# A hand-written order for every engine in an attention and maxout-FFN kernel, with padded queries and the first batch masked on VectorE

## The chip, the cores and the metric

The kernel runs on one core of a Trainium2 chip. The metric is the device time of one execution in microseconds, the median of several runs. "Span" is the first to the last instruction in the profiled execution; it is about 2 us shorter than the timed value.

## The reference, cut to what matters

```python
B, H, S, Nb, D = (8, 8, 576, 16, 64)          # causal attention, 16 beacon keys ahead of 576
scores = where(causal, -1e9, scale * q @ k_all^T)
attn   = softmax(scores) @ v_all              # 8 batches of 8 heads
x = attn.transpose(0, 2, 1, 3).reshape(4608, 512)
h = max(x @ w1, x @ w2, x @ w3)               # 768 wide
out = h @ w_out
```

Inputs and output are fp32; the kernel computes in bf16 with fp32 accumulation.

## The kernel before

Heads are taken in pairs. For one pair TensorE transposes q and k (12 and 16 small matmuls), then computes the scores k by q in 12 matmuls (six pieces, two heads). ScalarE takes the exponential out of PSUM, GpSimd writes zeros over the masked part, and after two pairs (a quad) TensorE runs six PV passes of 20 matmuls, each on a quarter of the array's columns. Part 0 of each half gives the softmax sums, which ScalarE turns into reciprocals with Ln and Exp. The FFN works on blocks of 512 tokens: 18 units of four matmuls (mm1) and four units of six (mm2). There are 32 pairs, 96 PV passes and 198 FFN units, and 4064 matmuls in all.

```python
def emit_scores(hp, q_sb, k_sb, at_sb, j0):
    # ... 12 transposes into qT_ps (score pool), VectorE copies to qT
    # ... 16 transposes into kT_ps (score pool), VectorE copies each head's half to a zero-padded kT
    for t in range(n_kt):
        for r0, r1 in groups:
            for e in range(2):
                nc.tensor.matmul(ps[...], kTf[e][...], qT[:, r0:r1, p0:QP], start=True, stop=True)
            for e in range(2):
                nc.scalar.activation(out=at_sb[...], in_=sc[e][...], func=AF.Exp, scale=scale)
        for e in range(2):
            nc.gpsimd.affine_select(out=view, in_=view, ...)     # causal mask, every batch
# ... emit_pv, emit_mm1, emit_mm2

loads = {0: emit_loads(0, H // 2)}       # every load is issued by GpSimd
emit_weight_loads()                      # 24 + 1 loads
loads[1] = emit_loads(1, 1)
for b in range(B):
    if b + 2 < B:
        loads[b + 2] = emit_loads(b + 2, 1)
    for g in range(2):
        # ... scores of two pairs, then emit_pv
    with tc.high_priority(offset=-(10**6)):        # the scheduler fills FFN in where it can
        for tb in blocks_after[b]:
            # ... mm2 of the block before, mm1 of this one
```

A scheduler fixes the order of each engine's instructions when the program is built, taking attention first and FFN where attention would wait. PSUM has three score buffers (also used by the transposes), two PV buffers and three FFN buffers.

The softmax here doesn't subtract the row's maximum and nothing guards it: scores larger than these inputs give would overflow.

## Time and profile before

| | before |
|---|---|
| timed, median of 3 | 419.08 us (418.48 to 420.77) |
| span | 417.2 us |
| TensorE busy | 365.0 us (87%) |
| next busiest, VectorE and ScalarE | 45%, 44% |

First, from the profile page of before, the busy time of each engine, and TensorE's busy share and granted clock in tenths over 40 equal slices of the span.

```profile
span 417.2 us, 9759 instructions
...
PE 365.0 (87%) x4024; PEld 187.9 (45%) x4064; DVE 188.4 (45%) x311; ACT 185.4 (44%) x503; POOL 170.8 (41%) x432
...
PE   3871159999999999999799999999999999999994
...
PEclk9999999999999999999999999999999999999998
...
```

TensorE's holes lie in the first seven slices. The windows view of before has three stretches: start-up, attention with FFN, FFN alone. Its columns are the stretch and its length, then busy microseconds (and instructions) of PE, PEld, DVE, ACT and POOL, then granted TensorE clock, DMA share and GB/s.

```profile
...
0.00:63.00 63.00, 29.56 (x279) 14.76 (x283) 12.84 (x24) 17.82 (x52) 48.62 (x97) 1.00 1.26 137
63.00:313.00 250.00, 237.50 (x3308) 128.94 (x3332) 122.86 (x211) 151.23 (x424) 122.17 (x336) 1.00 0.43 55
313.00:409.00 96.00, 94.79 (x434) 42.95 (x441) 50.00 (x74) 16.39 (x28) 0.00 (x0) 1.00 0.16 45
...
```

TensorE is the busy engine, but busy time is not streaming time: an FFN matmul is shown 380 ns long in the trace, and the next one starts after 216 ns. I therefore use the starts of successive matmuls. FFN to FFN is 216 ns at 512 (median). I count a matmul of N columns as N x 0.417 + 2.5 ns of streaming, a line that lies within 3 ns of all of these. A quarter of that counts for PV (in before, a group of four at 288 columns starts 122 ns ahead of the next group, and one at 234 columns 99 ns; the line gives 122.6 and 100.1), half for transposes (two of 96 columns in 43 ns, where the line gives 42.5); the medians of two PV or two transposes in a row lie within 13 ns of this count. By this count the whole kernel streams for 283 us. What a start-to-start time has beyond that I call a gap.

Next, the waits view of before for TensorE: who waited for whom, microseconds in total, how often, and the longest in microseconds.

```profile
...
PE sc L144 <- DMA q_sb<-in_q_dram: 12.8, 2, 8.1
PE pv L222 <- POOL at_sb L196: 9.2, 3, 7.3
PE sc L154 <- DMA k_sb<-in_beacon_k_dram: 4.9, 2, 3.6
...
```

The timeline of before at start-up, TensorE's and GpSimd's lines of it (start, duration, engine, line, operation; in brackets the idle time ahead and what ended it):

```profile
...
29.02 0.45 PE L178 MATMUL sc<-qT,kT_104 128*128 128x288 bf16 x1
29.25 0.45 PE L178 MATMUL sc<-qT,kT_106 128*128 128x288 bf16 x1
...
31.02 2.65 POOL L133 DMA_DIRECT2D v_sb<-in_v_dram  x3
...
37.20 0.88 POOL L133 DMA_DIRECT2D v_sb<-in_v_dram  x1 [3.53 <-DMA w_out_sb<-in_moe_w_out_dram]
...
40.63 0.69 PE L144 MATMUL sc<-ident,q_sb 96*64 96x96 bf16 x12 [8.11 <-DMA q_sb<-in_q_dram]
...
44.94 0.71 PE L154 MATMUL sc<-ident,k_sb 74*64 74x74 bf16 x16 [3.61 <-DMA k_sb<-in_beacon_k_dram]
...
46.08 0.78 POOL L114 DMA_DIRECT2D q_sb<-in_q_dram  x1 [4.47 <-issue]
...
54.10 0.73 POOL L133 DMA_DIRECT2D v_sb<-in_v_dram  x1 [1.85 <-DMA q_sb<-in_q_dram]
54.84 10.98 POOL L196 TENSOR_SCALAR_AFFINE_SELECT at_sb<-at_sb 128x114 bf16<-128x114 bf16 x40
55.26 0.67 PE L222 MATMUL pv<-at_sb,ones 128*32 128x288 bf16 x2 [7.28 <-POOL at_sb L196]
...
```

Between 32 and 55 us TensorE waits for batch 1's q, then its k, then for the mask of batch 0. In GpSimd's line the 40 selects of the mask (L196) stand behind its load issues for batches 1 and 2, which go on until 54.8 us. Between them are holes of 3.53 and 1.85 us that the trace puts down to earlier transfers; for the one of 4.47 us it names no cause.

### The profile page before, as it was taken

What the parts mean: (1) busy time and instruction counts of PE and PEld (TensorE: products, weight loads), DVE (VectorE), ACT (ScalarE), POOL (GpSimd) and SP (SyncE); (2) the same over time, 40 slices, a digit from 0 to 9 for tenths busy, and PEclk for the clock granted to TensorE, in tenths of its full rate; (3) what the DMA queues carried; (4) which work ended last, traced back from release to release, by engine and by line L of the source; (5) the groups of instructions that cost most, each with busy time, mean ns of one, the idle gap of its engine ahead of it and who ended that gap; (6) DMA issues with size and microseconds to landing.
All of it is one profiled execution on the core that took longest, in us unless ns stands there. A gap on an engine that the chain in (4) does not pass through costs nothing.

```text
span 417.2 us, 9759 instructions
## 1 busy us (share of the span) xinstructions
PE 365.0 (87%) x4024; PEld 187.9 (45%) x4064; DVE 188.4 (45%) x311; ACT 185.4 (44%) x503; POOL 170.8 (41%) x432
## 2 busy tenths in 40 slices
PE   3871159999999999999799999999999999999994
PEld 1430026545455454555545455455544444444441
DVE  3230103465354645545455363454545555555543
ACT  2661006565656557556574665755562121212120
POOL 8993588646625736644562523424230000000000
PEclk9999999999999999999999999999999999999998
DMA  7999996918729904960780300001200303030303
GB/s 97 146 173 177 123 109 90 88 20 112 53 64 148 61 2 62 125 91 6 116 58 11 93 3 2 2 2 39 65 2 2 101 0 102 0 101 2 101 0 102
DMA packets 61005, 27.65 MB, mean 66 GB/s; under 512 B 43168, under 2 KB 56352, under 8 KB 60960
## 3 DMA queue, kind: packets, MB, share of 16 engines
q0 software_dynamic: 55200, 17.58, 40.5%
q1 hardware_dynamic: 5760, 9.44, 8.0%
q8 instruction: 32, 0.52, 0.5%
q14 instruction: 13, 0.11, 0.1%
HBM read 35.13 MB, written 9.44 MB: 107 GB/s over the span
## 4 chain that ended last, share of the span: by engine, by line
PE 72%; POOL 9%; DMA 7%; ACT 5%; issue 3%; DVE 3%; SPq 0%; POOLq 0%; DVEq 0%
PE fps L248 33%; PE pv L222 13%; PE sc L178 12%; PE fps L266 11%; DMA k_sb<-in_k_dram 4%; ACT lnd L232 3%; POOL at_sb L196 3%; PE sc L144 2%; POOL v_sb L133 2%; POOL w_sb L99 2%; DMA q_sb<-in_q_dram 2%; DVE xT L237 2%; PE sc L154 1%; ACT recip L234 1%; DMA w_sb<-in_moe_w_dram 1%
## 5 line engine op out<-in xcount | busy, mean ns | idle before, releaser
L186 ACT ACTIVATE at_sb<-sc 128x288 bf16<-128x288 f32 (+4 forms) x384 | 129.1, 418 | 73.0 <-PE sc L178 70.5
L248 PE MATMUL fps<-xT,w_sb 128*128 128x512 bf16 x619 | 156.8, 380 | 3.3 <-issue 2.7
L196 POOL TENSOR_SCALAR_AFFINE_SELECT at_sb<-at_sb 128x132 bf16<-128x132 bf16 (+2 forms) x320 | 96.1, 324 | 107.1 <-ACT at_sb L186 101.1
L258 DVE TENSOR_TENSOR hT<-hT,fps 128x512 bf16<-128x512 bf16 x108 | 74.3, 688 | 77.2 <-PE fps L248 56.0
L248 PEld LDWEIGHTS <-w_sb 128*128 128x128 bf16 x648 | 60.9, 98 | 64.8 <-issue 3.6
L256 ACT CAST hT<-fps 128x512 bf16<-128x512 f32 x54 | 31.6, 584 | 86.7 <-PE fps L248 85.3
L222 PE MATMUL pv<-at_sb,v_sb 128*32 128x234 bf16 (+4 forms) x1280 | 62.1, 244 | 3.8 <-ACT lnd L232 2.4
L266 PE MATMUL fps<-w_out_sb,hT 128*128 128x512 bf16 x205 | 52.3, 379 | 2.2 <-issue 1.1
L222 PE MATMUL pv<-at_sb,ones 128*32 128x234 bf16 (+4 forms) x640 | 42.1, 249 | 11.8 <-POOL at_sb L196 9.2
L150 DVE COPY qT<-sc 128x576 bf16<-128x576 bf16 x32 | 14.6, 457 | 78.5 <-PE sc L144 73.7
L222 PEld LDWEIGHTS <-v_sb 128*32 128x32 bf16 (+1 forms) x1280 | 36.7, 98 | 15.4 <-issue 10.3
L237 DVE TENSOR_TENSOR xT<-pv,recip 128x288 bf16<-128x288 f32 x64 | 26.5, 453 | 37.4 <-ACT recip L234 36.4
L232 ACT ACTIVATE lnd<-pv 128x288 f32<-128x288 f32 x32 | 13.1, 410 | 58.0 <-PE pv L222 58.0
L133 POOL DMA_DIRECT2D v_sb<-in_v_dram x40 | 33.7, 860 | 8.2 <-DMA q_sb<-in_q_dram 4.6
L222 PEld LDWEIGHTS <-ones 128*32 128x32 bf16 (+1 forms) x640 | 20.6, 97 | 34.2 <-issue 27.0
L274 DVE COPY y<-fps 128x512 f32<-128x512 f32 x36 | 24.5, 691 | 23.1 <-PE fps L266 21.6
L144 PE MATMUL sc<-ident,q_sb 96*64 96x96 bf16 x384 | 20.7, 223 | 12.8 <-DMA q_sb<-in_q_dram 12.8
L266 PEld LDWEIGHTS <-hT 128*128 128x128 bf16 x216 | 20.4, 98 | 22.2 <-DVE hT L258 2.1
L154 PE MATMUL sc<-ident,k_sb 74*64 74x74 bf16 x512 | 20.5, 209 | 6.4 <-DMA k_sb<-in_beacon_k_dram 4.9
L144 PEld LDWEIGHTS <-q_sb 96*64 96x64 bf16 x384 | 13.2, 116 | 21.4 <-DMA q_sb<-in_q_dram 13.1
L178 PE MATMUL sc<-qT,kT_104 128*128 128x288 bf16 (+2 forms) x66 | 20.3, 308 | 1.8 <-DVE kT_104 L163 1.7
L178 PE MATMUL sc<-qT,kT_108 128*128 128x288 bf16 (+2 forms) x66 | 19.9, 301 | 1.8 <-DVE kT_108 L163 1.7
(38 smaller groups left out, 238.3 us busy)
## 6 DMA issues: line engine op xcount, KB each, us to landing
out_dram<-y SPq DMA_DIRECT2D x24, 192.0 KB, 2.4
q_sb<-in_q_dram POOLq DMA_DIRECT2D x7, 576.0 KB, 6.1
k_sb<-in_k_dram POOLq DMA_DIRECT2D x7, 576.0 KB, 9.7
v_sb<-in_v_dram POOLq DMA_DIRECT2D x24, 128.0 KB, 4.9
out_dram<-y SPq DMA_DIRECT2D x24, 128.0 KB, 2.4
w_sb<-in_moe_w_dram POOLq DMA_DIRECT2D x24, 96.0 KB, 4.0
out_dram<-y SPq DMA_DIRECT2D x24, 64.0 KB, 2.0
v_sb<-in_v_dram POOLq DMA_DIRECT2D x8, 112.0 KB, 4.0
```

Source lines behind the costliest of these rows:

```text
L133: nc.gpsimd.dma_start(out=v_sb[lo : lo + n, t], in_=v[b, :, t0 : t0 + n, :].rearrange("h p d -> p h d"),)
L144: nc.tensor.transpose(qT_ps[64 * e : 64 * e + 64, r, :], q_sb[:, h0 + e, r * D : (r + 1) * D], ident[0:QP, 0:QP],)
L178: nc.tensor.matmul(ps[0:n, 0 : nr * w].rearrange("k (r p) -> k r p", p=w), kTf[e][:, 128 * t : 128 * t + n], qT[:, r0:r1, p0:QP], start=Tr ...
L186: nc.scalar.activation(out=at_sb[0:n, t, j0 + e, r0:r1, p0:QP], in_=sc[e][0:n, 0 : nr * w].rearrange("k (r p) -> k r p", p=w), func=AF.Exp ...
L196: nc.gpsimd.affine_select(out=view, in_=view, compare_op=ALU.is_ge, fill=0.0, base=QR * p0 - k_tok[t], pattern=[[1, QR], [QR, p1 - p0]], c ...
L222: nc.tensor.matmul(ps[32 * j : 32 * j + 32, :, p0:QP], lhsT, at_sb[0:n, t, j, rs, p0:QP], start=(t == 0), stop=(t == n_kt - 1), tile_posit ...
L232: nc.scalar.activation(out=lnd, in_=ps, func=AF.Ln)
L237: nc.vector.tensor_mul(xs.rearrange("c (r p) -> c r p", p=QP), ps, recip)
L248: nc.tensor.matmul(ps, w_in[i][:, ct, 128 * ft : 128 * (ft + 1)], xT[:, ct, t0 : t0 + TOKB], start=(ct == 0), stop=(ct == n_ct - 1),)
L256: nc.scalar.copy(hT[:, ft, :], ps)
L258: nc.vector.tensor_max(hT[:, ft, :], hT[:, ft, :], ps)
L266: nc.tensor.matmul(ps, hT[:, ft, 128 * tt : 128 * (tt + 1)], w_out_sb[:, ft, :], start=(ft == 0), stop=(ft == n_ft - 1),)
```

## The change

The intent was to take the order out of the scheduler's hands: each step holds one score piece, then a burst of two PV passes if due, then the next pair's transposes if due, then FFN units. The transposes, PV and FFN stay in blocks. GpSimd is freed in the first batch, by masking on VectorE with a mask built once. The diff is cut to its core; comments behind # in it are mine.

```diff
+    with tc.manual_schedule():
+        emit_all()
...
     # now q is padded in two tiles and k copied once; before it was the other way round
+            nc.vector.tensor_copy(qz[p % NQZ][e][hs], qT_ps[hs])
+        nc.vector.tensor_copy(kT, kT_ps.rearrange("d r p -> d p r"))
...
+        if b == 0:
+            view = at_sb[0:n, t, j0 : j0 + 2, r0:r1, p0:p1]
+            m = mask[0:n, t, None, r0:r1, 0 : p1 - p0]
+            nc.vector.tensor_mul(view, view, m.to_broadcast([n, 2, nr, p1 - p0]))
+            return
...
-                for j in range(4):            # 24 weight loads of 96 KB
+            for j in range(4):                # 12 of 192 KB
...
+        load_weights()
+        load_qk(1, slice(0, H))
+        ...
+        for p in range(NPAIR):
+            b, pi = divmod(p, PPB)
+            for c in range(len(chunks)):                 # six steps a pair
+                emit_scores(p, c)
+                if p >= 2 and p % 2 == 0 and 1 <= c <= 3:
+                    emit_pv(p // 2 - 1, c - 1)           # two passes
+                if c == 4 and pi == 0:
+                    ready = b - 1                        # FFN of the batch before may start
+                if c == 4 and p + 1 < NPAIR:
+                    emit_transposes(p + 1)
+                if b > 0:
+                    allowed += 0.95
+                    while done[0] + 1 <= allowed and ... units[done[0]][0] <= ready:
+                        emit_ffn(ready, allowed)
+            ...  # loads of batch b + 1 after the pairs of batch b
```

In this order a batch's 22 units are used up at 0.95 a step before the batch ends, and the next 22 become available only at step 4 of the next batch's first pair. Credit piles up meanwhile, so four to nine units then come at once.

More of the change, by code (lines that the diff above doesn't have):

```diff
@@ L4 @@
 import concourse.tile as tile
-from concourse import bass_utils, mybir
+from concourse import mybir
 from concourse.masks import make_identity
@@ L56, with head @@
     p_min = [max(0, t0) // QR for t0 in k_tok]
+    p_max = [min(QP, -(-(k_tok[t] + k_rows[t]) // QR)) for t in range(n_kt)]
+    MW = max(p_max[t] - p_min[t] for t in range(n_kt))
     RH = QR // 2
-    const = ctx.enter_context(tc.tile_pool(name="const", bufs=1))
-    ident = const.tile([128, 128], BF16)
-    make_identity(nc, ident)
-    ones = const.tile([128, 32], BF16)
-    nc.vector.memset(ones, 1.0)
-    nc.scalar.preload_act_table_set("natural_log_exp_and_others")
+    HALF = RH * QP
+    n_quad = 2
+    NPAIR = B * H // 2
+    def head(g, j):
+        return n_quad * j + g
+    const = ctx.enter_context(tc.tile_pool(name="const", bufs=1))
     wpool = ctx.enter_context(tc.tile_pool(name="wpool", bufs=1))
@@ L72 @@
     load_pool = ctx.enter_context(tc.tile_pool(name="load", bufs=3))
-    qkt_pool = ctx.enter_context(tc.tile_pool(name="qkt", bufs=3))
+    kt_pool = ctx.enter_context(tc.tile_pool(name="kt", bufs=2))
     at_pool = ctx.enter_context(tc.tile_pool(name="at", bufs=2))
-    nrm_pool = ctx.enter_context(tc.tile_pool(name="nrm", bufs=3))
-    ffn_h = ctx.enter_context(tc.tile_pool(name="ffn_h", bufs=3))
+    nrm_pool = ctx.enter_context(tc.tile_pool(name="nrm", bufs=2))
+    ffn_h = ctx.enter_context(tc.tile_pool(name="ffn_h", bufs=2))
     ffn_y = ctx.enter_context(tc.tile_pool(name="ffn_y", bufs=3))
@@ L80 @@
     ffn_psum = ctx.enter_context(tc.tile_pool(name="ffn_psum", bufs=3, space=PSUM))
-    kT_bufs = []
-    for i in range(3):
+    ident = const.tile([128, 128], BF16)
+    make_identity(nc, ident)
+    ones = const.tile([128, 32], BF16)
+    nc.vector.memset(ones, 1.0)
+    nc.scalar.preload_act_table_set("natural_log_exp_and_others")
+    NQZ = 2
+    qz = []
+    for i in range(NQZ):
         pair = []
         for e in range(2):
-            z = const.tile([128, KP, KR], BF16, name=f"kT{i}{e}")
+            z = const.tile([128, QR, QP], BF16, name=f"qz{i}{e}")
@@ L88 @@
             nc.vector.memset(z[64 * (1 - e) : 64 * (1 - e) + 64], 0.0)
             pair.append(z)
-        kT_bufs.append(pair)
-    n_pairs = [0]
-    def emit_weight_loads():
-        for i, w_ap in enumerate((moe_w1, moe_w2, moe_w3)):
-            wv = w_ap.rearrange("(g j e c) f -> g j c e f", g=2, j=4, e=2, c=32)
-            for g in range(2):
-                for j in range(4):
-                    nc.gpsimd.dma_start(
-                        out=w_in[i][32 * j : 32 * j + 32, 2 * g : 2 * g + 2, :],
-                        in_=wv[g, j],
-                    )
+        qz.append(pair)
@@ new lines, with load_tiles, load_qk @@
+    tiles = {}
+    def load_tiles(b):
+        if b not in tiles:
+            tiles[b] = (
+                load_pool.tile([QP, H, QR * D], BF16, name="q_sb"),
+                load_pool.tile([KP, H, KR * D], BF16, name="k_sb"),
+                load_pool.tile([128, n_kt, H, D], BF16, name="v_sb"),
+            )
+        return tiles[b]
+    def load_qk(b, hs):
+        q_sb, k_sb, _ = load_tiles(b)
+        nc.gpsimd.dma_start(
+            out=q_sb[:, hs, :], in_=q[b, hs].rearrange("h (p r) d -> p h (r d)", r=QR)
+        )
+        nc.gpsimd.dma_start(
+            out=k_sb[BP:KP, hs, :],
+            in_=k[b, hs].rearrange("h (p r) d -> p h (r d)", r=KR),
+        )
+        nc.gpsimd.dma_start(
+            out=k_sb[0:BP, hs, :],
+            in_=beacon_k[b, hs].rearrange("h (p r) d -> p h (r d)", r=KR),
+        )
@@ new lines, in load_v, with load_weights @@
+    def load_v(b, t):
+        v_sb = load_tiles(b)[2]
+        lo = 0
+        if t == 0:
+            lo = Nb
+            nc.gpsimd.dma_start(
+                out=v_sb[0:Nb, 0], in_=beacon_v[b].rearrange("h n d -> n h d")
+            )
+        t0 = k_tok[t] + lo
+        n = k_rows[t] - lo
+        nc.gpsimd.dma_start(
+            out=v_sb[lo : lo + n, t],
+            in_=v[b, :, t0 : t0 + n, :].rearrange("h p d -> p h d"),
+        )
+    def load_weights():
+        for i, w_ap in enumerate((moe_w1, moe_w2, moe_w3)):
+            wv = w_ap.rearrange("(j t c) f -> j c t f", t=n_ct, c=32)
+            for j in range(4):
+                nc.gpsimd.dma_start(out=w_in[i][32 * j : 32 * j + 32], in_=wv[j])
@@ L105, in emit_weight_loads, with build_mask, emit_transposes @@
         )
-    def emit_loads(b, split):
-        q_sb = load_pool.tile([QP, H, QR * D], BF16, name="q_sb")
-        k_sb = load_pool.tile([KP, H, KR * D], BF16, name="k_sb")
-        v_sb = load_pool.tile([128, n_kt, H, D], BF16, name="v_sb")
-        step = H // split
-        for s in range(split):
-            hs = slice(s * step, (s + 1) * step)
-            nc.gpsimd.dma_start(
-                out=q_sb[:, hs, :],
-                in_=q[b, hs].rearrange("h (p r) d -> p h (r d)", r=QR),
-            )
-            nc.gpsimd.dma_start(
-                out=k_sb[BP:KP, hs, :],
-                in_=k[b, hs].rearrange("h (p r) d -> p h (r d)", r=KR),
-            )
-            nc.gpsimd.dma_start(
-                out=k_sb[0:BP, hs, :],
-                in_=beacon_k[b, hs].rearrange("h (p r) d -> p h (r d)", r=KR),
-            )
-        nc.gpsimd.dma_start(
-            out=v_sb[0:Nb, 0], in_=beacon_v[b].rearrange("h n d -> n h d")
-        )
-        for t in range(n_kt):
-            lo = Nb if t == 0 else 0
-            t0 = k_tok[t] + lo
-            n = k_rows[t] - lo
-            nc.gpsimd.dma_start(
-                out=v_sb[lo : lo + n, t],
-                in_=v[b, :, t0 : t0 + n, :].rearrange("h p d -> p h d"),
-            )
-        return q_sb, k_sb, v_sb
-    def emit_scores(hp, q_sb, k_sb, at_sb, j0):
-        h0 = 2 * hp
+    mask = const.tile([128, n_kt, QR, MW], BF16, name="mask")
+    nc.vector.memset(mask, 1.0)
+    def build_mask(t):
+        nc.gpsimd.affine_select(
+            out=mask[:, t],
+            in_=mask[:, t],
+            compare_op=ALU.is_ge,
+            fill=0.0,
+            base=QR * p_min[t] - k_tok[t],
+            pattern=[[1, QR], [QR, MW]],
+            channel_multiplier=-1,
+        )
+    state = {}
+    def emit_transposes(p):
+        b, pi = divmod(p, H // 2)
+        g, j0 = pi // 2, 2 * (pi % 2)
+        q_sb, k_sb, _ = load_tiles(b)
         qT_ps = sc_psum.tile([128, QR, QP], BF16, name="sc")
@@ L145, in emit_scores @@
                     qT_ps[64 * e : 64 * e + 64, r, :],
-                    q_sb[:, h0 + e, r * D : (r + 1) * D],
+                    q_sb[:, head(g, j0 + e), r * D : (r + 1) * D],
                     ident[0:QP, 0:QP],
                 )
-        qT = qkt_pool.tile([128, QR, QP], BF16, name="qT")
-        nc.vector.tensor_copy(qT, qT_ps)
         kT_ps = sc_psum.tile([128, KR, KP], BF16, name="sc")
@@ L155, in emit_scores @@
                     kT_ps[64 * e : 64 * e + 64, r, :],
-                    k_sb[:, h0 + e, r * D : (r + 1) * D],
+                    k_sb[:, head(g, j0 + e), r * D : (r + 1) * D],
                     ident[0:KP, 0:KP],
                 )
-        kTf = []
         for e in range(2):
             hs = slice(64 * e, 64 * e + 64)
-            kT = kT_bufs[n_pairs[0] % 3][e]
-            nc.vector.tensor_copy(kT[hs], kT_ps[hs].rearrange("d r p -> d p r"))
-            kTf.append(kT.rearrange("d p r -> d (p r)"))
@@ L165, in emit_scores @@
-        n_pairs[0] += 1
+            nc.vector.tensor_copy(qz[p % NQZ][e][hs], qT_ps[hs])
+        kT = kt_pool.tile([128, KP, KR], BF16, name="kT")
+        nc.vector.tensor_copy(kT, kT_ps.rearrange("d r p -> d p r"))
+        state[p] = kT.rearrange("d p r -> d (p r)")
+    chunks = [(0, 0, RH), (0, RH, QR)] + [(t, 0, QR) for t in range(1, n_kt)]
+    def emit_scores(p, c):
+        b, pi = divmod(p, H // 2)
+        g, j0 = pi // 2, 2 * (pi % 2)
+        if c == 0 and j0 == 0:
+            state["at", p // 2] = at_pool.tile([128, n_kt, 4, QR, QP], BF16, name="at_sb")
+        at_sb = state["at", p // 2]
+        t, r0, r1 = chunks[c]
+        n = k_rows[t]
+        p0 = p_min[t]
+        w = QP - p0
+        nr = r1 - r0
+        kT = state[p]
+        sc = []
+        for e in range(2):
+            ps = sc_psum.tile([128, 512], FP32, name="sc")
+            sc.append(ps)
+            nc.tensor.matmul(
+                ps[0:n, 0 : nr * w].rearrange("k (r p) -> k r p", p=w),
+                kT[:, 128 * t : 128 * t + n],
+                qz[p % NQZ][e][:, r0:r1, p0:QP],
+                start=True,
+                stop=True,
+            )
+        for e in range(2):
+            nc.scalar.activation(
+                out=at_sb[0:n, t, j0 + e, r0:r1, p0:QP],
+                in_=sc[e][0:n, 0 : nr * w].rearrange("k (r p) -> k r p", p=w),
+                func=AF.Exp,
+                scale=scale,
+            )
+        p1 = p_max[t]
+        if b == 0:
[3 more added lines that the diff above has]
+            return
+        for e in range(2):
+            view = at_sb[0:n, t, j0 + e, r0:r1, p0:p1]
+            nc.gpsimd.affine_select(
+                out=view,
+                in_=view,
+                compare_op=ALU.is_ge,
+                fill=0.0,
+                base=QR * p0 + r0 - k_tok[t],
+                pattern=[[1, nr], [QR, p1 - p0]],
+                channel_multiplier=-1,
+            )
@@ L167, in emit_scores, with pv_pass @@
+    def pv_pass(b, g, v_sb, at_sb, hf, part):
+        rs = slice(hf * RH, (hf + 1) * RH)
+        ps = pv_psum.tile([128, RH, QP], FP32, name="pv")
         for t in range(n_kt):
@@ L169, in emit_scores @@
             p0 = p_min[t]
-            w = QP - p0
-            groups = [(0, RH), (RH, QR)] if QR * w > 512 else [(0, QR)]
-            for r0, r1 in groups:
-                nr = r1 - r0
-                sc = []
-                for e in range(2):
-                    ps = sc_psum.tile([128, 512], FP32, name="sc")
-                    sc.append(ps)
-                    nc.tensor.matmul(
-                        ps[0:n, 0 : nr * w].rearrange("k (r p) -> k r p", p=w),
-                        kTf[e][:, 128 * t : 128 * t + n],
-                        qT[:, r0:r1, p0:QP],
-                        start=True,
-                        stop=True,
-                    )
-                for e in range(2):
-                    nc.scalar.activation(
-                        out=at_sb[0:n, t, j0 + e, r0:r1, p0:QP],
-                        in_=sc[e][0:n, 0 : nr * w].rearrange("k (r p) -> k r p", p=w),
-                        func=AF.Exp,
-                        scale=scale,
-                    )
@@ L193, in emit_scores @@
-            p1 = min(QP, -(-(k_tok[t] + n) // QR))
-            for e in range(2):
-                view = at_sb[0:n, t, j0 + e, :, p0:p1]
-                nc.gpsimd.affine_select(
-                    out=view,
-                    in_=view,
-                    compare_op=ALU.is_ge,
-                    fill=0.0,
-                    base=QR * p0 - k_tok[t],
-                    pattern=[[1, QR], [QR, p1 - p0]],
-                    channel_multiplier=-1,
-                )
-    def emit_pv(b, g, v_sb, at_sb):
-        for hf in range(2):
-            rs = slice(hf * RH, (hf + 1) * RH)
-            c0 = b * S + hf * RH * QP
-            recip = None
-            for part in range(3):
-                ps = pv_psum.tile([128, RH, QP], FP32, name="pv")
-                for t in range(n_kt):
-                    n = k_rows[t]
-                    p0 = p_min[t]
-                    for j in range(4):
-                        if part == 0:
-                            lhsT = ones[0:n, :]
-                        else:
-                            d0 = 32 * (part - 1)
-                            lhsT = v_sb[0:n, t, 4 * g + j, d0 : d0 + 32]
-                        nc.tensor.matmul(
-                            ps[32 * j : 32 * j + 32, :, p0:QP],
-                            lhsT,
-                            at_sb[0:n, t, j, rs, p0:QP],
-                            start=(t == 0),
-                            stop=(t == n_kt - 1),
-                            tile_position=(0, 32 * j),
-                        )
-                if part == 0:
-                    lnd = nrm_pool.tile([128, RH, QP], FP32, name="lnd")
-                    nc.scalar.activation(out=lnd, in_=ps, func=AF.Ln)
-                    recip = nrm_pool.tile([128, RH, QP], FP32, name="recip")
-                    nc.scalar.activation(out=recip, in_=lnd, func=AF.Exp, scale=-1.0)
-                else:
-                    xs = xT[:, 2 * g + part - 1, c0 : c0 + RH * QP]
-                    nc.vector.tensor_mul(
-                        xs.rearrange("c (r p) -> c r p", p=QP), ps, recip
-                    )
@@ L241, in emit_mm1 @@
-    def emit_mm1(tb):
-        t0 = tb * TOKB
-        hT = ffn_h.tile([128, n_ft, TOKB], BF16, name="hT")
+            for j in range(4):
+                if part == 0:
+                    lhsT = ones[0:n, :]
+                else:
+                    d0 = 32 * (part - 1)
+                    lhsT = v_sb[0:n, t, head(g, j), d0 : d0 + 32]
+                nc.tensor.matmul(
+                    ps[32 * j : 32 * j + 32, :, p0:QP],
+                    lhsT,
+                    at_sb[0:n, t, j, rs, p0:QP],
+                    start=(t == 0),
+                    stop=(t == n_kt - 1),
+                    tile_position=(0, 32 * j),
+                )
@@ new lines, in pv_pass @@
+        if part == 0:
+            lnd = nrm_pool.tile([128, RH, QP], FP32, name="lnd")
+            nc.scalar.activation(out=lnd, in_=ps, func=AF.Ln)
+            recip = nrm_pool.tile([128, RH, QP], FP32, name="recip")
+            nc.scalar.activation(out=recip, in_=lnd, func=AF.Exp, scale=-1.0)
+            state["recip", hf] = recip
+        else:
+            c0 = b * S + hf * HALF
+            xs = xT[:, 2 * g + part - 1, c0 : c0 + HALF]
+            nc.vector.tensor_mul(
+                xs.rearrange("c (r p) -> c r p", p=QP), ps, state["recip", hf]
+            )
@@ new lines, with emit_pv, mm1_unit @@
+    PV_ORDER = [(0, 0), (0, 1), (0, 2), (1, 0), (1, 1), (1, 2)]
+    def emit_pv(quad, step):
+        b, g = divmod(quad, n_quad)
+        at_sb = state["at", quad]
+        for hf, part in PV_ORDER[2 * step : 2 * step + 2]:
+            pv_pass(b, g, load_tiles(b)[2], at_sb, hf, part)
+    hTs = {}
+    def mm1_unit(tb, ft, i, pool, name):
+        t0 = tb * TOKB
+        if ft == 0 and i == 0:
+            hTs[tb] = ffn_h.tile([128, n_ft, TOKB], BF16, name="hT")
+        hT = hTs[tb]
+        ps = pool.tile([128, TOKB], FP32, name=name)
+        for ct in range(n_ct):
+            nc.tensor.matmul(
+                ps,
+                w_in[i][:, ct, 128 * ft : 128 * (ft + 1)],
+                xT[:, ct, t0 : t0 + TOKB],
+                start=(ct == 0),
+                stop=(ct == n_ct - 1),
+            )
+        if i == 0:
+            nc.scalar.copy(hT[:, ft, :], ps)
+        else:
+            nc.vector.tensor_max(hT[:, ft, :], hT[:, ft, :], ps)
@@ new lines, in mm2_unit @@
+    def mm2_unit(tb, tt, pool, name):
+        hT = hTs[tb]
+        c0 = tb * TOKB + 128 * tt
+        ps = pool.tile([128, d_model], FP32, name=name)
+        for ft in range(n_ft):
+            nc.tensor.matmul(
+                ps,
+                hT[:, ft, 128 * tt : 128 * (tt + 1)],
+                w_out_sb[:, ft, :],
+                start=(ft == 0),
+                stop=(ft == n_ft - 1),
+            )
+        y = ffn_y.tile([128, d_model], FP32, name="y")
+        nc.vector.tensor_copy(y, ps)
+        c = c0
+        while c < c0 + 128:
+            b, rem = divmod(c, S)
+            r, p = divmod(rem, QP)
+            n = min(QP - p, c0 + 128 - c)
+            row = b * S + QR * p + r
+            nc.sync.dma_start(
+                out[row : row + QR * (n - 1) + 1 : QR, :], y[c - c0 : c - c0 + n, :]
+            )
+            c += n
@@ L244, in emit_mm1 @@
+    units = []
+    for tb in range(n_tokb):
+        last_b = (TOKB * (tb + 1) - 1) // S
         for ft in range(n_ft):
             for i in range(3):
-                ps = ffn_psum.tile([128, TOKB], FP32, name="fps")
-                for ct in range(n_ct):
-                    nc.tensor.matmul(
-                        ps,
-                        w_in[i][:, ct, 128 * ft : 128 * (ft + 1)],
-                        xT[:, ct, t0 : t0 + TOKB],
-                        start=(ct == 0),
-                        stop=(ct == n_ct - 1),
-                    )
@@ L255, in emit_mm1 @@
-                if i == 0:
-                    nc.scalar.copy(hT[:, ft, :], ps)
-                else:
-                    nc.vector.tensor_max(hT[:, ft, :], hT[:, ft, :], ps)
-        return hT
-    def emit_mm2(tb, hT):
-        for tt in range(TOKB // 128):
-            c0 = tb * TOKB + 128 * tt
-            ps = ffn_psum.tile([128, d_model], FP32, name="fps")
-            for ft in range(n_ft):
-                nc.tensor.matmul(
-                    ps,
-                    hT[:, ft, 128 * tt : 128 * (tt + 1)],
-                    w_out_sb[:, ft, :],
-                    start=(ft == 0),
-                    stop=(ft == n_ft - 1),
-                )
-            y = ffn_y.tile([128, d_model], FP32, name="y")
-            nc.vector.tensor_copy(y, ps)
-            c = c0
-            while c < c0 + 128:
-                b, rem = divmod(c, S)
-                r, p = divmod(rem, QP)
-                n = min(QP - p, c0 + 128 - c)
-                row = b * S + QR * p + r
-                nc.sync.dma_start(
-                    out[row : row + QR * (n - 1) + 1 : QR, :], y[c - c0 : c - c0 + n, :]
-                )
-                c += n
@@ L287 @@
-    blocks_after = {b: [] for b in range(B)}
-    for tb in range(n_tokb):
-        blocks_after[(TOKB * (tb + 1) - 1) // S].append(tb)
-    loads = {0: emit_loads(0, H // 2)}
-    emit_weight_loads()
-    loads[1] = emit_loads(1, 1)
-    pending = None
-    for b in range(B):
-        if b + 2 < B:
-            loads[b + 2] = emit_loads(b + 2, 1)
-        q_sb, k_sb, v_sb = loads.pop(b)
-        for g in range(2):
-            at_sb = at_pool.tile([128, n_kt, 4, QR, QP], BF16, name="at_sb")
-            for hp in (2 * g, 2 * g + 1):
-                emit_scores(hp, q_sb, k_sb, at_sb, 2 * (hp % 2))
-            emit_pv(b, g, v_sb, at_sb)
-        with tc.high_priority(offset=-(10**6)):
-            for tb in blocks_after[b]:
-                if pending is not None:
-                    emit_mm2(*pending)
-                pending = (tb, emit_mm1(tb))
@@ L309, with emit_ffn, emit_all @@
-    emit_mm2(*pending)
+                units.append((last_b, mm1_unit, (tb, ft, i)))
+        for tt in range(TOKB // 128):
+            units.append((last_b, mm2_unit, (tb, tt)))
+    done = [0]
+    def emit_ffn(ready, limit, pool=None, name="fps"):
+        if done[0] < min(limit, len(units)) and units[done[0]][0] <= ready:
+            _, fn, args = units[done[0]]
+            fn(*args, pool or ffn_psum, name)
+            done[0] += 1
+    def emit_all():
+        PPB = H // 2
+        for pi in range(2):
+            g, j0 = pi // 2, 2 * (pi % 2)
+            load_qk(0, slice(head(g, j0), head(g, j0 + 1) + 1, n_quad))
+        for t in range(n_kt):
+            load_v(0, t)
+            build_mask(t)
+        for pi in range(2, PPB):
+            g, j0 = pi // 2, 2 * (pi % 2)
+            load_qk(0, slice(head(g, j0), head(g, j0 + 1) + 1, n_quad))
+        load_weights()
+        load_qk(1, slice(0, H))
+        for t in range(n_kt):
+            load_v(1, t)
+        ready = -1
+        allowed = 0.0
+        emit_transposes(0)
+        for p in range(NPAIR):
[10 more added lines that the diff above has]
+                    allowed += 0.95
+                    while done[0] + 1 <= allowed and done[0] < len(units) and units[done[0]][0] <= ready:
+                        emit_ffn(ready, allowed)
+            if b >= 1 and b + 1 < B:
+                if pi == 0:
+                    load_qk(b + 1, slice(0, H))
+                elif pi < 3:
+                    for t in range(0, 3) if pi == 1 else range(3, n_kt):
+                        load_v(b + 1, t)
+            if pi == PPB - 1 and b > 0:
+                tiles.pop(b - 1)
+        for step in range(3):
+            emit_ffn(B - 2, len(units))
+            emit_pv(NPAIR // 2 - 1, step)
+        i = 0
+        tail = [(ffn_psum, "fps"), (sc_psum, "sc"), (pv_psum, "pv")]
+        while done[0] < len(units):
+            pool, name = tail[i % 3]
+            emit_ffn(B - 1, len(units), *tail[i % 2])
+            i += 1
```

## The prediction

> **What bounds it now.** The page shows TensorE busy 87% of 417.2 us, next engines 45%. The windows view splits the span in three.
> - 0 to 63 us, start-up. The timeline shows TensorE stopping at 32.3 us for batch 1's q (transposes at 40.6) and k (44.9), then until 55.3 us for batch 0's mask: GpSimd, in order, issues the loads of batches 1 and 2 (28 to 54.8 us) before its 40 selects. Bandwidth is 178 GB/s in 20 to 40 us, so the data of batch 0, weights and batch 1 drain at about that rate.
> - 63 to 313 us, mixed: TensorE busy 95%, but that hides gaps. From start-to-start times of single matmuls, 70 to 310 us holds 163 us of streaming (N columns at 216 ns per 512, column-quartered PV at a quarter) and some 70 us of extra time, nearly all at changes of kind: scores to PV 108 ns, PV to FFN 188, PV to scores 181, transposes to FFN 312, PV to transposes 152, transposes to PV 218. [...]
> - 313 to 409 us, FFN alone: 216 ns each, dense.
>
> **What the change does.** TensorE's instructions are the same 4064, in another order. The built order's counts of changes, times the costs above, give about 70 us before and 40 us after (transposes/PV alternations 116 to none; PV-scores entries 84 to 46). Interleaving single score matmuls with FFN matmuls mattered little (7 and 23 ns).
> Batch 0's mask moves to VectorE (24 multiplies; I estimate 0.35 us each from the 0.45 us of similar ones), and batch 2's loads come after batch 1's first scores, so the wait at 47.5 to 55.3 us and slow PV to 62 us disappears. The wait for batch 1's q and k stays: the same roughly 6 MB precede them, and the hand order puts batch 1's transposes ahead of everything else. With 12 instead of 24 weight loads (0.57 us issue each) I expect k at about 43 us instead of 44.9, first batch-1 scores near 44.7 us. Start-up gain: about 20 us of work already done.
> q copies to two padded tiles, k once: VectorE 1.7 us a pair instead of 2.0, off the path.
>
> **What it adds.** In-order stalls. FFN units run out before each batch's end and until step 4 of the next batch's first pair (credit 0.95 a step, 22 units a batch), then come in bursts of 4 to 9. Starved steps are bound by ScalarE: exps of 0.24 to 0.58 us, Ln and reciprocal 0.85 us a pass, about 10 us against 6.5 us of TensorE work late in the kernel. I estimate 24 us in all, plus 8 us for k transposes waiting for a score buffer (0.3 to 0.4 us a pair). Before has almost none of this.
>
> **Sum.** 44.7 + 273 streaming left + 40 changes + 32 stalls + about 9 of tail and output = 399 us of span, about 400 us timed. Predicted 399 us, range 385 to 411. Faster 0.83, same 0.14, slower 0.03.
>
> **Signs.** Right: no TensorE wait for GpSimd's batch-0 mask; TensorE idle some 10 us before about 43 us on DMA; FFN-only tail about 43 us instead of 97; 40 us in changes of kind; ScalarE near full in the starved steps at each batch's start. Start-up wrong: first batch-1 scores not at 43 to 46 us. Stalls wrong: TensorE waits inside batches 1 to 7 not near 32 us.
>
> **What would make it wrong.** Loads arriving much earlier or later; stalls per pair twice my estimate (then about 415); or none (then about 375).

## The result, and the profile after

The changed kernel took 373.2 us (372.74 to 373.75, 4 runs) against 418.78 us (4 runs) of before in the same rounds. The ratio is 0.89, 95% interval 0.8875 to 0.8925. A ratio here is the mean time of one kernel's fast runs over that of the other's of the same rounds, so it is not quite the ratio of the quoted medians. The result is 26 us below the predicted 399 us and outside the range of 385 to 411. From the profile page of the changed kernel, the same lines as above:

```profile
span 371.0 us, 9819 instructions
...
PE 333.5 (90%) x4064; PEld 178.9 (48%) x4064; DVE 185.9 (50%) x334; ACT 186.2 (50%) x503; POOL 163.9 (44%) x441
...
PE   2895499999999998989997999799998999899994
...
PEclk9996599999999999989998999989998999999998
...
```

The clock row has dips. Those in the start-up are not new, since score matmuls of before run at half rate there too (0.23 us from start to start in place of 0.12), whatever its row says; those in four later slices are, and they come back in experiment 5. The windows view of the changed kernel, cut where batch 1's first scores start and where the FFN is alone:

```profile
...
0.00:44.30 44.30, 25.29 (x308) 13.31 (x309) 17.47 (x49) 18.84 (x53) 28.80 (x51) 0.84 1.22 151
44.30:324.30 280.00, 266.57 (x3564) 146.94 (x3564) 145.55 (x252) 160.38 (x438) 135.10 (x390) 0.97 0.49 67
324.30:366.00 41.70, 41.66 (x204) 18.69 (x192) 22.16 (x34) 7.02 (x12) 0.00 (x0) 1.00 0.14 38
...
```

The waits view of the changed kernel for TensorE:

```profile
...
PE sc L176 <- DMA q_sb<-in_q_dram: 9.5, 2, 4.8
PE sc L215 <- DVE kT L193: 7.1, 9, 1.1
PE sc L215 <- ACT at_sb L223: 6.4, 20, 0.6
PE sc L184 <- DMA k_sb<-in_beacon_k_dram: 4.7, 2, 3.3
PE sc L184 <- ACT at_sb L223: 1.4, 4, 0.4
...
```

No wait for GpSimd is left. The FFN alone takes 42 us at the end instead of 96. The timeline of the changed kernel at start-up, TensorE alone:

```profile
...
33.62 0.34 PE L215 MATMUL sc<-qz_110,kT 128*128 128x210 bf16 x1
38.71 0.69 PE L176 MATMUL sc<-ident,q_sb 96*64 96x96 bf16 x12 [4.75 <-DMA q_sb<-in_q_dram]
42.73 0.70 PE L184 MATMUL sc<-ident,k_sb 74*64 74x74 bf16 x16 [3.33 <-DMA k_sb<-in_beacon_k_dram]
...
44.30 0.42 PE L215 MATMUL sc<-qz_104,kT 128*128 128x288 bf16 x1 [0.58 <-DVE kT L193]
...
```

These are batch 1's q transposes, k transposes and first scores; I had written 43 us for k and 44.7 us for the scores. The times of the start-up were therefore as predicted (no run separates what the fewer weight loads gave of it), and so was the streaming left after it (273 us). What was wrong lies in the gaps. The following ledger is worked out from the profiled runs, in microseconds. It is counted from the start of batch 1's first transpose. "Changes" are gaps between matmuls of different kinds (FFN, scores, PV, transposes); "within" are gaps between two of the same kind. The number in brackets counts the changes into and out of PV and transposes, so without scores to FFN and back, where the median gap is under 1 ns in both traces.

| | starts at | streaming left | changes | within | last matmul to end | span |
|---|---|---|---|---|---|---|
| before | 40.6 | 275.4 | 63.6 (337) | 32.1 | 5.4 | 417.2 |
| changed | 38.7 | 273.3 | 17.8 (141) | 35.7 | 5.5 | 371.0 |

The trace of before lacks 40 of the 4064 matmul records. All 40 are FFN matmuls, and each shows as a gap of 200 to 460 ns beside an FFN matmul; there are exactly 40 such gaps, and 216 ns is taken off each here. The trace of the changed kernel has all 4064. The groups view by shape shows it, with the count after the x. Of before:

```profile
...
L248 PE MATMUL fps<-xT,w_sb 128*128 128x512 bf16 x619 | 156.8, 380 | 3.3 <-issue 2.7 <-DVE hT L258 0.2
L266 PE MATMUL fps<-w_out_sb,hT 128*128 128x512 bf16 x205 | 52.3, 379 | 2.2 <-issue 1.1 <-DVE hT L258 0.8
...
```

And of the changed kernel, where the scores' pool carries some of the FFN in the tail:

```profile
...
L300 PE MATMUL fps<-xT,w_sb 128*128 128x512 bf16 x576 | 140.4, 380 | 0.0
L317 PE MATMUL fps<-w_out_sb,hT 128*128 128x512 bf16 x192 | 46.5, 380 | 0.0
...
L300 PE MATMUL sc<-xT,w_sb 128*128 128x512 bf16 x72 | 18.5, 379 | 0.0
...
L317 PE MATMUL sc<-w_out_sb,hT 128*128 128x512 bf16 x24 | 5.8, 379 | 0.0
...
```

The sums are 619 + 205 = 824 before and 576 + 192 + 72 + 24 = 864 after, and 864 is what the program holds. In 21 of the 24 places where before goes from transposes to FFN, the missing record is the first FFN matmul. The recorded gap there is 336 to 346 ns. In the three places with all records it is 110 to 112 ns, and in the changed kernel it is 110 ns (median of 22).

### The profile page after: what moved, and what is told of

Its sections match the earlier page's. It is cut to its first block, busy times and chain, and to the rows that moved or that the text cites. A ratio compares the mean times of both kernels' runs of the same rounds, so it can differ in the third digit from the quotient of the medians.

```text
span 371.0 us, 9819 instructions
## 1 busy us (share of the span) xinstructions
PE 333.5 (90%) x4064; PEld 178.9 (48%) x4064; DVE 185.9 (50%) x334; ACT 186.2 (50%) x503; POOL 163.9 (44%) x441
## 4 chain that ended last, share of the span: by engine, by line
PE 75%; ACT 7%; DMA 7%; POOL 6%; DVE 2%; issue 1%; POOLq 0%; ACTq 0%
PE fps L300 35%; PE fps L317 11%; PE sc L215 10%; PE pv L261 10%; PE sc L300 4%; ACT at_sb L223 4%; DMA k_sb<-in_beacon_k_dram 4%; PE sc L184 3%; PE sc L176 2%; DMA w_sb<-in_moe_w_dram 2%; PE sc L317 1%; POOL v_sb L137 1%; DVE kT L193 1%; ACT lnd L271 1%; DMA v_sb<-in_v_dram 1%
## 5 line engine op out<-in xcount | busy, mean ns | idle before, releaser
L239 POOL TENSOR_SCALAR_AFFINE_SELECT at_sb<-at_sb 128x57 bf16<-128x57 bf16 (+1 forms) x336 | 94.3, 300 | 145.2 <-ACT at_sb L223 139.7
L300 PE MATMUL fps<-xT,w_sb 128*128 128x512 bf16 x576 | 140.4, 380 | 0.0
L310 DVE TENSOR_TENSOR hT<-hT,fps 128x512 bf16<-128x512 bf16 x96 | 65.9, 686 | 56.9 <-PE fps L300 42.8
L215 PEld LDWEIGHTS <-kT 128*128 128x128 bf16 (+1 forms) x384 | 36.6, 105 | 52.1 <-DVE kT L193 11.9
L317 PE MATMUL fps<-w_out_sb,hT 128*128 128x512 bf16 x192 | 46.5, 380 | 0.0
L137 POOL DMA_DIRECT2D v_sb<-in_v_dram x40 | 33.9, 851 | 6.0 <-DMA w_out_sb<-in_moe_w_out_dram 2.6
L261 PE MATMUL pv<-at_sb,v_sb 128*32 128x288 bf16 (+4 forms) x1280 | 36.0, 254 | 0.3 <-ACT lnd L271 0.2
L215 PE MATMUL sc<-qz_104,kT 128*128 128x288 bf16 (+2 forms) x96 | 30.2, 317 | 5.4 <-DVE kT L193 5.4
L261 PEld LDWEIGHTS <-v_sb 128*32 128x32 bf16 (+1 forms) x1280 | 27.5, 103 | 15.3 <-issue 13.0
L215 PE MATMUL sc<-qz_106,kT 128*128 128x288 bf16 (+2 forms) x96 | 30.0, 313 | 3.1 <-ACT at_sb L223 2.8
L215 PE MATMUL sc<-qz_110,kT 128*128 128x288 bf16 (+2 forms) x96 | 28.6, 298 | 4.0 <-ACT at_sb L223 3.5
L215 PE MATMUL sc<-qz_108,kT 128*128 128x288 bf16 (+2 forms) x96 | 28.8, 301 | 2.3 <-DVE kT L193 1.7
L193 DVE COPY kT<-sc 128x592 bf16<-128x592 bf16 x32 | 24.8, 775 | 5.1 <-PE sc L184 4.2
L184 PE MATMUL sc<-ident,k_sb 74*64 74x74 bf16 x512 | 15.8, 205 | 6.1 <-DMA k_sb<-in_beacon_k_dram 4.7
L261 PE MATMUL pv<-at_sb,ones 128*32 128x288 bf16 (+4 forms) x640 | 20.4, 260 | 1.0 <-DVE xT L278 0.8
```

The source lines that it names most:

```text
L137: nc.gpsimd.dma_start(out=v_sb[lo : lo + n, t], in_=v[b, :, t0 : t0 + n, :].rearrange("h p d -> p h d"),)
L184: nc.tensor.transpose(kT_ps[64 * e : 64 * e + 64, r, :], k_sb[:, head(g, j0 + e), r * D : (r + 1) * D], ident[0:KP, 0:KP],)
L193: nc.vector.tensor_copy(kT, kT_ps.rearrange("d r p -> d p r"))
L215: nc.tensor.matmul(ps[0:n, 0 : nr * w].rearrange("k (r p) -> k r p", p=w), kT[:, 128 * t : 128 * t + n], qz[p % NQZ][e][:, r0:r1, p0:QP], ...
L239: nc.gpsimd.affine_select(out=view, in_=view, compare_op=ALU.is_ge, fill=0.0, base=QR * p0 + r0 - k_tok[t], pattern=[[1, nr], [QR, p1 - p0 ...
L261: nc.tensor.matmul(ps[32 * j : 32 * j + 32, :, p0:QP], lhsT, at_sb[0:n, t, j, rs, p0:QP], start=(t == 0), stop=(t == n_kt - 1), tile_posit ...
```

## The experiments

Nine versions were run, one of them twice. All gave correct results. "Changed" is the kernel of the section before.

### 1. The start-up alone: VectorE mask in the kernel before

```diff
+            if b == 0:
+                view = at_sb[0:n, t, j0 : j0 + 2, :, p0:p1]
+                m = mask[0:n, t, None, :, 0 : p1 - p0]
+                nc.vector.tensor_mul(view, view, m.to_broadcast([n, 2, QR, p1 - p0]))
+                continue
             for e in range(2):
                 ...  # affine_select, as before; the mask is built once, ahead of the weight loads
```

> The kernel before, its scheduler's order kept, with the first batch masked on VectorE only. Theory (the start-up gain comes from the mask no longer queued behind GpSimd's loads): 403 to 412, first batch-1 scores still at about 46 us, no 7 us TensorE wait for GpSimd. Rival (the wait for batch 1's k hides it): 415 to 419.

402.32 us against 418.32 us in the same rounds (ratio 0.9616, 0.9587 to 0.9645). The time is 0.7 us below the range of the theory, and the wait for GpSimd is gone. One detail is not as expected: the scheduler, with batch 0 complete, put FFN ahead of batch 1, as TensorE's timeline of this version shows.

```profile
...
42.61 8.76 PE L253 MATMUL fps<-xT,w_sb 128*128 128x512 bf16 x37
51.29 0.45 PE L144 MATMUL sc<-ident,q_sb 96*64 96x96 bf16 x12
...
```

So batch 1's transposes and scores came after 51 us, not at 46, and the wait for its data was filled with FFN of batch 0. In the scheduler's order this is worth 16 us. Not all of it need be the start-up: the scheduler, given other times, also made 307 changes of kind in place of 337 (see the last ledger).

### 2. The order with the old mask: GpSimd masks batch 0

```diff
-        if b == 0:
+        if False:
```

> The changed kernel with the first batch masked on GpSimd again. Theory (mask of batch 0 stands behind batch 1's loads, until 39 us, and the hand order makes TensorE wait for it before batch 0's third pair): 384 to 395. Rival (start-up is bounded by batch 1's data in either case): 373 to 377.

386.74 us (ratio to before 0.9241, 0.9219 to 0.9263), so 13.5 us more than the changed kernel: the theory holds. In its trace GpSimd's first select starts at 40.1 us, after the load issues, and TensorE waits 18.5 us for it in one piece. Together, 1 and 2 divide the gain. The start-up is worth 16.0 us in the old order and 13.5 us in the new. The new order is worth 29.1 us with the VectorE mask (402.3 to 373.2) and 31.6 us without. My prediction had about 20 us for the start-up and, for the order, 30 us fewer changes against 32 us of new stalls: nothing.

### 3. The price of a change of kind, by itself

One unneeded transpose, whose result nothing reads, in the middle of each of the 44 FFN units of the tail:

```diff
         for ct in range(n_ct):
+            if extra and ct == 2:
+                extra[0]()      # nc.tensor.transpose(scr[0:64, 0, 0:96], ident..., ident...)
             nc.tensor.matmul(
```

> The changed kernel with one unneeded transpose put in the middle of each of the 44 FFN units of the tail, where nothing else waits: 88 more changes of kind. If a change costs what the trace of the changed kernel shows (FFN to transpose about 95 ns, transpose to FFN 110 ns): about 10 us more, 381 to 385. If it costs what I took from the trace of before in the prediction (94 and 312 ns): about 19 us more, 390 to 394.

384.22 us, 11.0 us above the changed kernel (both beside runs of before that agree within 0.5 us). That is 250 ns for the way in, the transpose and the way out. In its trace FFN to transpose has 93 ns of gap and transpose to FFN 141 ns (medians; this trace too lacks records, 44 of FFN matmuls). The price in my prediction, 94 + 312 ns, is refuted. The 312 ns was 110 ns and, mostly, a record that was not there.

### 4. The same price in the mixed phase

This one builds on the version of experiment 7. Each pair of PV passes goes into an FFN unit, one after its first and one after its third matmul, in place of ahead of it; instructions and buffers are the same.

```diff
         for ct in range(n_ct):
+            if hooks and ct in (1, 3):
+                pv_pass(*hooks.pop(0))
             nc.tensor.matmul(
```

> The best version (even spread, batch 1's q and k ahead of the weights) with each pair of PV passes put inside an FFN unit, after its first and third matmul, in place of ahead of it: the same instructions and tiles, 78 more changes of kind in the mixed phase. At 93 to 112 ns a change as in the changed kernel's trace: 8 us more, 358 to 361. If changes are hidden behind other waits there and cost nothing: within 2 us of the best version. At the costs of my prediction (FFN to PV 101, PV to FFN 188): 11 us more, 362 to 365.

360.34 us (5 runs) against 351.75 us: 8.6 us for 78 more changes, 110 ns each. (By the ledger below the changes themselves cost 7.9 us more, 101 ns each; batch 1 also started 0.7 us later.) In its trace FFN to PV is 93 ns and PV to FFN 112 ns at nearly every one of 81 places. The rival, that a change hides behind other waits, falls. What TensorE does in these 93 to 112 ns no run shows.

### 5. FFN units spread evenly

```diff
                 if c == 4 and pi == 0:
                     ready = b - 1
+                    allowed = float(done[0])
...
-                    allowed += 0.95
+                    allowed += 22.0 / 24.0 + 1e-6
```

> The changed kernel with the 22 FFN units of a batch spread evenly over its 24 steps (credit reset when a batch becomes ready, 22/24 a step) in place of bursts and starved steps; nothing else. Theory A (the waits that the changed kernel still has sit in the starved steps: score buffers held by ScalarE, k copy, and half-rate TensorE after them): 373 falls to 347 to 358, the extra time in scores-to-scores gaps (17 us now) falls below 6 us. Rival (the waits come from the in-order queue at every pair, wherever the FFN stands): 366 or more.

Timed runs: 357.66 to 359.44 us (ratio 0.8563). The profiled execution fell into the slow state, 479.99 us with a mean granted clock of 0.666, so nothing is compared with it. The kernel was run again for a profile:

> The evenly spread kernel once more, unchanged, because its profiled run fell in the slow state: 357 to 360 again. Of the changed kernel's 54 us of extra time after batch 1's first transpose, theory A (starved steps) expects the gaps within scores, PV and transposes (35 us) to fall by 12 to 18 us and the changes of kind to stay near 18 us; the rival (fewer changes are what the even spread brings) expects the changes to fall instead.

358.58 us (358.57 to 358.81), 14.6 us below the changed kernel, half a microsecond above the range I had expected. From the ledger: changes 17.6 us, where the changed kernel has 17.8 (145 of them), and 21.7 us within a kind instead of 35.7. Theory A holds in kind, and the 14.0 us in the ledger lie within its 12 to 18; both rivals are refuted. One expectation failed: the gaps from scores to scores, counted from batch 1's first transpose, fell from 18.8 to 9.1 us and not below 6.

What a starved step costs can be read in the changed kernel's timeline. For comparison, two PV passes of batch 0 in the same trace:

```profile
...
47.69 0.55 PE L261 MATMUL pv<-at_sb,v_sb 128*32 128x288 bf16 x20
48.07 0.53 PE L261 MATMUL pv<-at_sb,ones 128*32 128x288 bf16 x20
...
```

And the steps ahead of the burst of FFN in batch 5, the burst itself last:

```profile
...
198.80 0.20 PE L215 MATMUL sc<-qz_110,kT 128*80 128x84 bf16 x1 [0.33 <-ACT at_sb L223]
199.87 0.30 PE L215 MATMUL sc<-qz_104,kT 128*128 128x288 bf16 x1 [0.87 <-DVE kT L193]
...
200.73 0.28 PE L215 MATMUL sc<-qz_106,kT 128*128 128x288 bf16 x1 [0.31 <-ACT at_sb L223]
200.94 0.89 PE L261 MATMUL pv<-at_sb,ones 128*32 128x288 bf16 x20
201.65 0.88 PE L261 MATMUL pv<-at_sb,v_sb 128*32 128x288 bf16 x20
...
207.06 6.22 PE L300 MATMUL fps<-xT,w_sb 128*128 128x512 bf16 x28
...
```

The windows view of the changed kernel there (the third column from the right is the granted clock):

```profile
...
195.00:200.00 5.00, 3.41 (x43) 1.87 (x42) 2.99 (x5) 2.75 (x8) 2.44 (x8) 1.00 0.68 184
200.00:205.00 5.00, 4.69 (x88) 2.65 (x86) 0.92 (x2) 3.39 (x9) 1.70 (x6) 0.66 0.00 0
...
```

The same stretches of the evenly spread kernel:

```profile
...
195.00:200.00 5.00, 5.00 (x97) 2.85 (x96) 2.93 (x6) 2.66 (x6) 1.32 (x4) 1.00 0.39 99
200.00:205.00 5.00, 4.68 (x51) 2.53 (x50) 2.74 (x5) 2.66 (x9) 3.15 (x7) 1.00 0.42 99
...
```

With no FFN to fill in, the scores wait 0.87 us for VectorE's copy of k and 0.31 us for a score buffer that ScalarE still reads. Then the granted clock falls to 0.66 in this stretch, and two PV passes start 0.71 us apart instead of 0.38. That second cost does not appear among the waits, because TensorE counts as busy (4.69 of the 5 us): the waits view of the changed kernel from 45 us on lists 11 us, while the gaps within a kind come to 30 us there. (Not all of this difference is the clock. A wait is counted only from the modelled end of the matmul before, and a score matmul of 288 columns is shown as 0.29 us long where the next can start after 0.12.) The prediction has no such cost.

The windows view bounds the clock's part. In the changed kernel the granted clock is 0.50 or 0.51 in four stretches of 3.4 us, from 160.0, 200.9, 241.9 and 282.9 us; the evenly spread kernel has 1.00 from 49.4 to 356 us. Four such stretches at half rate lose at most 6.8 us, an estimate from these figures. So about half of the 14.0 us at most was the clock, and the rest was waits. In the 3.4 us ahead of each stretch TensorE was busy for 1.8 to 2.0 us.

### 6. Padding k instead of q, in the new order

The two padded tiles keep their name in the list and take the shape of k.

```diff
-            nc.vector.tensor_copy(qz[p % NQZ][e][hs], qT_ps[hs])
-        nc.vector.tensor_copy(kT, kT_ps.rearrange("d r p -> d p r"))
+        nc.vector.tensor_copy(qT, qT_ps)
+            nc.vector.tensor_copy(qz[p % NQZ][e][hs], kT_ps[hs].rearrange("d r p -> d p r"))
```

> The changed kernel with k padded in two tiles and q copied once, as before. My prediction put this off the critical path: 373 to 376. If the padding of q matters (the k copy, which the next pair's first scores wait for, is one of 0.78 us in place of two): 378 or more.

372.72 us: the same as the changed kernel's 373.2. The padding of q does nothing for the time here.

### 7. Batch 1's q and k ahead of the weights, with the even spread

```diff
-        load_weights()
         load_qk(1, slice(0, H))
+        load_weights()
...
-                if c == 4 and pi == 0:
+                if (pi, c) == ((1, 0) if b == 1 else (0, 4)):
...
-                    allowed += 0.95
+                    allowed += (1.0 if b == 1 else 22.0 / 24.0) + 1e-6
```

> Even spread, and batch 1's q and k loaded ahead of the weights, FFN of batch 0 starting one pair later. If the start-up is bounded by bytes ahead of batch 1's q and k: first batch-1 transposes at 28 to 34 us in place of 38.7, no half-rate stretch, 349 to 354. If the wait only moves to the weights: 356 to 360.

351.75 us (ratio 0.8395), 6.8 us below the even spread. Batch 1's first transposes start at 33.0 us in place of 38.8, when TensorE has just finished with the pair before, so they no longer wait. That is 5.8 us of the 6.8; the later start of batch 0's FFN was changed with it, and no run separates the two. The half-rate stretch stays, though: the timeline shows PV passes still 0.71 us apart, at 36.80 and 37.51 us. That part of my expectation was wrong.

### 8. The k transposes in another PSUM pool

```diff
-        kT_ps = sc_psum.tile([128, KR, KP], BF16, name="sc")
+        kT_ps = ffn_psum.tile([128, KR, KP], BF16, name="fps")
```

> The best version with the k transposes written into the FFN's PSUM pool instead of the scores' pool. If the gaps inside the transposes (11 us in the best version's trace) are the wait for a score buffer that ScalarE still reads: 342 to 347, those gaps under 3 us. If a shorter supply of FFN buffers takes it back: 350 or more.

342.89 us (342.62 to 342.98, 5 runs; ratio to before 0.8183, 0.8157 to 0.8208). The gaps within the transposes fall from 11.0 to 0.8 us, and the whole by 8.9 us. This is the fastest version. The waits view for TensorE shows it. First the version of experiment 7, whose pool was still the old one:

```profile
...
PE sc L184 <- ACT at_sb L223: 5.4, 15, 0.4
...
PE sc L215 <- ACT at_sb L223: 4.4, 14, 0.3
...
```

And this version:

```profile
...
PE sc L215 <- ACT at_sb L223: 0.7, 3, 0.3
```

The transposes (L184) no longer wait for ScalarE. A part of the gain moved elsewhere: the waits of scores for the copy of k grew from 5.4 to 8.5 us, and in the ledger below the changes grew by 4.3 us while the gaps within a kind fell by 13.9.

### 9. The written order without a scheduler

```diff
+    ctx.enter_context(tc.manual_schedule())
     loads = {0: emit_loads(0, H // 2)}
```

on the version of experiment 1.

> The kernel before with the VectorE mask for the first batch, issued in the order in which it is written, without the scheduler: 87 changes between FFN, scores, PV and transposes instead of about 307, but no FFN beside the scores. If the number of changes alone set the time: 375 or less. If the filling of the waits matters as much: 430 to 500.

502.24 us, one run of unknown state, with a mean granted clock of 0.794. It has 76 recorded changes after batch 1's first transpose, yet 79 us of gaps within scores and 34 us within PV. Its granted clock is below full for long (0.63 from 59 to 100 us), so a part of these gaps may be the clock, which no run separates. The slow state of experiment 5 is not the explanation: the median from FFN to FFN is 216 ns here and 357 ns in that slow run. By this one run, few changes are worth nothing if the waits are not filled.

The ledger of these versions in one place, in microseconds:

| | starts at | streaming left | changes | within | span |
|---|---|---|---|---|---|
| before, VectorE mask | 51.3 | 262.7 | 53 (307) | 28 | 399.6 |
| changed | 38.7 | 273.3 | 17.8 (141) | 35.7 | 371.0 |
| even spread | 38.8 | 273.3 | 17.6 (145) | 21.7 | 356.9 |
| and q, k of batch 1 first | 33.0 | 273.3 | 15.7 (145) | 22.4 | 350.0 |
| that, PV inside FFN units | 33.7 | 273.3 | 23.6 (223) | 21.7 | 357.9 |
| that, k transposes in the FFN pool | 33.9 | 273.3 | 20.0 (145) | 8.5 | 341.2 |

The last row builds on the fourth, not on the fifth. In the first row 37 of that trace's 41 missing records could be placed, so its two gap columns are rounded. The first four columns, with about 5.5 us after the last matmul, make up the span.

## Why the prediction was right or wrong

**Right in its times, high in its gain: the start-up.** The wait for GpSimd's mask is gone, and batch 1's first scores came at 44.3 us (44.7 predicted). Experiments 1 and 2 put the start-up at 13.5 to 16 us; I had said about 20.

**Right: the streaming (273 us), the padding of q off the path (experiment 6) and the direction of the change.**

**Wrong: "The built order's counts of changes, times the costs above, give about 70 us before and 40 us after".** This is the step that failed. In the changed kernel the changes came to 17.8 us. The counts were about right and the prices were not. The sum also cannot be had from the prices that the text lists: the six large ones give about 20 us for the new order. A mean gap of 49 ns for every scores-to-scores pair and 23 ns for every FFN-to-scores pair, both from the old trace, bring it to about 32 us. The first of these is not a change of kind (the ledger has it under "within"), and I charged the same kind of wait again under stalls. The second has a median of 0 in the changed kernel.

Among the listed prices, transposes to FFN (312 ns) held a missing record nearly every time and is 110 ns. The other large ones (PV to FFN 188, PV to scores 181, transposes to PV 218) were means over a schedule that cut PV bursts up. In the changed kernel their medians are 112 ns, 113 ns and none.

The old trace shows where the difference for PV lies: the gap from PV to FFN depends on how wide the last PV matmul is. It is 107 to 113 ns after 42 columns, where a pass ends, 161 or 162 ns after 168, 171 to 182 ns after 234 and 185 to 199 ns after 288, three places with a missing record left out. The changed kernel leaves PV only at the end of a pass. (My estimate of a reason, from the line through the starts above, which no run tests: a PV matmul is counted at a quarter of its streaming, and the last one has nothing behind it to hide the other three quarters, 15 ns at 42 columns and 92 at 288; this difference of 77 ns compares with 73 to 87 measured.)

Experiments 3 and 4 confirm 100 to 120 ns a change, apart from any scheduler, for PV passes that are left whole. The term of the changes (40 us said, 17.8 measured) is 22 of the 28 us between the predicted and the measured span.

**Nearly right in size, for a reason only partly right: the stalls.** I wrote 24 us for starved steps and 8 us for the k transposes. After 45 us the gaps within a kind are 30 us. The transposes' part was 4.7 us then; with the even spread and the loads moved, 8.9 us was to be had from them (experiment 8). The even spread recovered 14.6 us; that leaves the 24 us too high, and a part of what it recovered was the clock, which I had not counted. "Starved steps are bound by ScalarE" did not hold either: the sign was ScalarE near full, and it was busy 2.75 and 3.39 us of the 5 us from 195 and from 200 us (the fourth busy time in the windows lines of experiment 5). The prediction also said that no stalls at all would give about 375 us. That 373.2 us lies near it is luck: the stalls were there, and it was the changes that cost less.

**Wrong: "Before has almost none of this".** The old order has 32 us of gaps within a kind, about as many as the new one, though some 11 us of it is in the start-up. The net of the order was predicted as 30 us gained against 32 us lost. It was 35 us fewer in changes and 8 us more within a kind (the version of experiment 1 against the changed kernel).

**A little wrong: the end.** I had 9 us after the FFN's streaming; from the last matmul's start to the end it was 5.5 us, as in before (5.4).

What stays open: why the clock falls in the starved steps of the late batches (TensorE was busy for 1.8 to 2.0 us of the 3.4 us before, and no single wait after 45 us was longer than 0.9 us, but that the short waits are the cause is not shown), why one execution of the evenly spread kernel ran at a granted clock of 0.65 from about 50 us to its end (479.99 us instead of 358; what else the chip was doing then is not known), and how much of the remaining 8.5 us within a kind is bound to the pair's copies. No run separates these.

## What to carry to other kernels

When TensorE is the busiest engine, count its start-to-start times against streaming time: here 283 us of streaming stood in a span of 417 us. Keep each PV pass whole and the transposes in a block (medians here of 93 to 95 ns of gap on the way into them and 109 to 141 ns on the way out, but under 1 ns between scores and FFN) while spreading the filler work evenly, since both the number of changes and the starved steps cost time, and few changes alone were a loss (502 us). Before pricing anything from gaps in a trace, compare the number of records with the number of instructions in the program, and look at where a burst was cut: here a pass of PV cut in its middle cost up to 199 ns to leave, and 112 ns at its end.
